# Moving head tails across partitions with a TensorE permutation instead of a DMA, with fewer filler matmuls and a new instruction order, in a fused linear-attention and feed-forward kernel

## The chip, the cores and the metric

The kernel runs on one core of a Trainium2 chip. The metric is the device time in microseconds of one execution, and lower is better. Several executions are timed; the median is given together with the lowest and the highest. One further execution is recorded by the hardware profiler, and all views below come from it. Engines are named as the profile names them: PE is TensorE (its matmuls), PEld its weight loads, DVE is VectorE, ACT is ScalarE, POOL is GpSimd, and SP is SyncE, which here only starts DMAs.

## The reference

Eight batches of eight heads, 576 positions and a head width of 64 go through a linear attention with a learned feature map. The result goes through a layer norm and a two-layer feed-forward block with a residual.

```python
def phi(x):
    proj = np.einsum('bhsd,df->bhsf', x, w_phi)            # 64 -> 128 features
    proj = proj - np.max(np.abs(proj), axis=-1, keepdims=True)
    return np.concatenate([np.exp(proj), np.exp(-proj)], axis=-1)
q_p, k_p = (phi(q), phi(k))
kv = np.einsum('bhsf,bhsd->bhfd', k_p, v)
z = np.sum(k_p, axis=2)
num = np.einsum('bhsf,bhfd->bhsd', q_p, kv)
den = np.einsum('bhsf,bhf->bhs', q_p, z)[..., None] + 1e-06
attn_out = num / den
...
# x: attn_out with the heads side by side, 8 x 576 x 512
mu = np.mean(x, axis=-1, keepdims=True)
var = np.mean((x - mu) ** 2, axis=-1, keepdims=True)
xn = (x - mu) / np.sqrt(var + 1e-06) * g_ln
ch = np.maximum(xn @ w_ch1, 0.0) @ w_ch2                   # 512 -> 2048 -> 512
return x + ch
```

## The kernel before

Work is tiled by pairs of batches. A pair has 1152 positions, which fill nine tiles of 128 rows. Tiles 0 to 7 hold 512 positions of each batch. Tile 8 is the mixed tile: its upper 64 rows are the last 64 positions of the first batch, its lower 64 rows those of the second. There are four pairs and 32 attention units, eight for each pair. A unit covers two (batch, head) combinations at once, one on each half of the partitions. For the first two pairs (`SPLIT`) a unit holds two neighbouring heads of the same batch; for the last two pairs it holds the same head of both batches.

A unit runs like this. Its q, k and v are loaded by SP (line 509, called by `load_main` and `load_tails`; the tails are the last 64 positions). q and k are transposed: for units 0 to 7 by PE (lines 645 and 653) with copies from PSUM by DVE or ACT (lines 660 and 662), from unit 8 on by a cast on DVE, ACT or POOL (lines 706 to 712, tile `b`) and a DMA transpose on SP (line 731). PE forms the projections `pk` (line 796), `pq` and `pt` and, for the tails, `px` (lines 754 and 755). DVE takes the row maxima `m`, ACT the exponentials `eb`, `ea` and `em`. v is scaled by an exponential into `vv` (lines 824 to 837), on POOL, or for the first units on POOL or DVE. PE accumulates the state in `n_bank` (lines 993 and 998), DVE or ACT copies it to `KV`, PE forms `num` (lines 1041 and 1047), DVE adds the two halves into `numc` (lines 1055 and 1060) and takes the reciprocal `rden` (line 1064), and POOL writes the quotient to `x` (line 1070).

In a unit of the first two pairs both heads belong to one batch, so on the mixed tile one of the two results comes out on the wrong half of the partitions. POOL writes that result to a small tile `xs`; after every fourth unit one DMA on ACT's queue (line 1130) moves the four collected results, 64 rows by 256 columns, to the other half of `x`. There are four such moves, two for each of the first two pairs.

When a pair's rows are complete, DVE takes the layer norm statistics (lines 1188 and 1203), the centred rows `xc` are transposed to `xT` (PE for the first pair, with g multiplied in through `ngln` at lines 1161 and 1163; DMA after that), and the feed-forward block runs. It is 832 matmuls for the hidden layer (`hT_ps`, line 1275), a relu on DVE or ACT (lines 1283 and 1285), 592 matmuls for the output (`ch_ps`, line 1305) and a final addition on DVE (line 1312).

The weights are loaded on POOL's queue, w1 in four parts at line 601 and w2 in four parts at line 612. Two small DMAs on SP (line 521) wait for a part of w1 or of w2, so that the loads behind them on SP start only then. g is loaded by SP at line 591, and DVE makes `ngln` of it at line 595.

The program order of every engine is written by a planner, the class `Order`. Each operation is added with its engine (or a choice of engines), an estimated duration, what it reads and writes, and the buffers that it takes or gives back. `run` plays the operations through in estimated time, and each engine takes the ready operation of lowest rank. A rank is a due time, worked back from the end, plus a correction from the table `OFF` for each kind of operation and unit. When PE has nothing ready before 36 us of planned time (`WARM`), the planner puts in a filler, a matmul of zeros with 120 columns (line 1503). A full DMA ring (`RING`) holds back further DMAs on it. The engines then run their lists strictly in this order.

PSUM has three pools: A (two buffers of two banks), N (one bank, `n_bank`, which the fillers write too) and B (three banks, for transposes, projections, `hT_ps` and `ch_ps`).

Of the kernel before, what the change touches and what calls it, by code (L numbers as in the profile page):

```python
# [10 lines left out]
FP32 = mybir.dt.float32  # L11
# [6 lines left out]
def bcast(ap: bass.AP, dim: int, n: int) -> bass.AP:  # L18
# [11 lines left out]
        0: 32.4, 1: -3.7, 2: 184.2, 3: -840, 4: -194.1, 5: -28.3, 6: -229.5, 7: 33.3, 8: 45,  # L30
        9: -539.6, 10: 152, 11: 166.5, 12: 510.5, 13: 780.4, 14: 17,
    },
    "gln": {
        0: -336.4,
    },
    "k": {
        0: -747.6, 1: 3.1, 2: 13.2, 3: 2336.4, 4: -153, 5: 169.6, 6: 3041.1, 7: -24.5, 8: -13.7,
        9: -121.2, 10: 2105.3, 11: -111.4, 12: -801.7, 13: 48.4, 14: 956.1,
    },
    "k.copy": {  # L40
        0: 303.5, 1: -156.1, 2: -30.4, 3: -67.5, 4: -25.5, 5: -23.1, 6: -8.4, 7: 126.8,
    },
    "k.em": {
        0: -36.2, 1: 16, 2: -30.2, 3: 2074.1, 4: -160.9, 5: 506.5, 6: 1498.1, 7: -115.7, 8: 487.3,
        9: -248.4, 10: -509.2, 11: -763.6, 12: 32.9, 13: -16.4, 14: 333.1,
    },
    "k.exp": {
        0: 892, 1: 680.1, 2: 913.8, 3: 1000, 4: -396.5, 5: 114.6, 6: 959.1, 7: 128.1, 8: 314.6,
        9: 1536.5, 10: -354.9, 11: -335.4, 12: -27, 13: -77, 14: 237.3,
    },  # L50
    "k.max": {
        0: -6661.7, 1: -16.8, 2: -277.6, 3: 22.3, 4: -472.7, 5: -30.2, 6: -31.4, 7: -186.7,
        8: -308.3, 9: -143.6, 10: -195.1, 11: 155.1, 12: -6149.9, 13: -3.3, 14: -6158.9,
    },
    "k.trans": {
        0: -97.2, 1: 108, 2: -53.9, 3: -186.6, 4: -480.3, 5: -159.3, 6: -450, 7: -38.7,
    },
    "kv": {
        0: 286.2, 1: 1059.8, 2: -466.3, 3: -37.1, 4: -180.5, 5: -17.5, 6: -549.1, 7: -227.7,
        8: -245.7, 9: -33.9, 10: -8.1, 11: 346.1, 12: 907.8, 13: -19.5, 14: -60.7,  # L60
    },
    "kv.copy": {
        0: 912.4, 1: 169, 2: 1552.3, 3: -226.4, 4: 572, 5: 112, 6: 1240.8, 7: 572, 8: 491.8,
        9: 1311.2, 10: 40.2, 11: 221.2, 12: 24.5, 13: -502.8, 14: 73.8,
    },
    "ln": {
        1: 301.8, 3: -104.9, 5: -6.6, 7: 128.2, 9: -561.5, 11: -849.4, 12: -1099, 13: 116.3,
        14: 10.6,
    },
    "load": {  # L70
        0: 158.8,
    },
    "mixed": {
        0: 35.8, 1: -185.8, 2: -16.9, 3: -86.7, 4: -229.1, 5: 195.3, 6: -90.5, 7: 455.9, 8: -949.2,
        9: -967.5, 10: -91.5, 11: 16.1, 12: 77.2, 13: -6043, 14: 448.4,
    },
    "mixed.exp": {
        0: 20.9, 1: 560.6, 2: 91.1, 3: -306.6, 4: 197, 5: -2.3, 6: 42.5, 7: 349.4, 8: 228.3,
        9: -167.6, 10: -376.7, 11: -109.3, 12: -155.8, 13: -167, 14: -28.1,
    },  # L80
    "mixed.max": {
        0: 65.3, 1: 102.8, 2: -327.8, 3: -962.8, 4: 211.4, 5: -1323, 6: 70.6, 7: -650, 8: 75.3,
        9: 1099.5, 10: 76.1, 11: -1098.5, 12: -90.7, 13: -715.7, 14: 529.6,
    },
    "num0": {
        0: 345.1, 1: -40.2, 2: -11.4, 3: 18, 4: -37.1, 6: 362.8, 7: 57.4, 8: 256.8, 9: -843.9,
        10: -49.5, 11: 591.4, 12: -1.8, 13: 963.9, 14: 184.1,
    },
    "num0.dve": {
        0: 101.2, 1: 2.8, 2: -67.5, 3: -245.5, 4: -32.1, 5: 407.7, 6: -61.4, 7: -245.2, 8: -405.8,  # L90
        9: -204.4, 10: 56.2, 11: 489.8, 12: -114.3, 13: -325.9, 14: -110.7,
    },
    "num0.put": {
        0: 415.1, 1: 56.4, 2: 23.3, 3: -82.8, 4: -553.5, 5: 481.8, 6: -1293.1, 7: 537.7, 8: -981,
        9: -845.9, 10: 128.5, 11: 74.2, 12: -1101.2, 13: 119.7, 14: -246.6,
    },
    "num1": {
        0: 1678.7, 1: 1611.5, 2: 204.2, 3: 8.1, 4: -173.6, 5: 22.3, 6: 448.5, 7: 1975.8, 8: -222.6,
        9: -54.5, 10: 13.7, 11: 39.8, 12: -1141.5, 13: -1220.2, 14: -1219,
    },  # L100
    "num1.dve": {
        0: 288.8, 1: 926.9, 2: 211.1, 3: 221.7, 4: -1480.5, 5: -121.2, 6: 7.4, 7: -321.5,
        8: -264.8, 9: -62.1, 10: -560, 11: -967, 12: -331.4, 13: -26.7, 14: 939.8,
    },
    "num1.put": {
        0: 763.2, 1: -18.1, 2: 211.3, 3: 3058.9, 4: 838.4, 5: 1781.7, 6: -13.1, 7: 830.5, 8: 749.5,
        9: 49.1, 10: -25.4, 11: 87.7, 12: -236.9, 13: 795.2, 14: 1071.9,
    },
    "q.copy": {
        0: 1413.7, 1: 594.3, 2: 486.8, 3: 263.7, 4: -71, 5: 12.4, 6: 148.6, 7: 195.7,  # L110
    },
    "q.em": {
        4: -274.3, 5: 1, 6: 27.6, 7: -502.7, 8: 29.8, 9: -502.3, 10: 65.2, 11: 494.7, 12: 761.6,
        13: 1224.5, 14: 52.8,
    },
    "q.max": {
        4: -11.4, 5: 178.1, 6: 2151.8, 7: -154.8, 8: 854.1, 9: -335.3, 10: 1738.2, 11: 296.6,
        12: -21.8, 13: -86.3, 14: 690.3,
    },
    "q.trans": {  # L120
        0: 136.7, 1: 242.2, 2: 16.5, 3: 122.9, 4: -6.8, 5: -19.6, 6: 91.3, 7: 27.9,
    },
    "q0": {
        0: 24.3, 1: 192.3, 2: 8.4, 3: -594.7,
    },
    "q0.em": {
        0: 34.4, 1: -74.9, 2: -376.1, 3: -208.6,
    },
    "q0.max": {
        0: 164.5, 1: 12.7, 2: 98.9, 3: -1420,  # L130
    },
    "q1": {
        0: -2210.5, 1: 15, 2: 17, 3: 1136.9,
    },
    "q1.em": {
        0: 2888.2, 1: -0.8, 2: 325.4, 3: 521.5,
    },
    "q1.max": {
        0: 360.6, 1: -0.1, 2: -2.6, 3: -49.7,
# [1401 lines left out]
```

## Time and profile before

| | us |
|---|---|
| median of 6 runs | 374.86 |
| lowest and highest | 373.31 and 377.55 |
| the profiled execution | 374.56 |
| its span, first to last instruction | 372.8 |
| first feed-forward matmul starts (line 1275) | 35.9 |
| first w2 load is issued (line 612) | 40.93 |
| last feed-forward matmul starts | 367.9 |
| four moves of `xs`, issue to landing | 3.3 to 5.1 |

The profile gives busy time for each engine; a "busy" PE is not a PE at its peak, since the ends of the pipelined matmuls are modelled. The chain of waits starts from the last instruction and is followed back, at each step to what released it or to the instruction before it on its engine. A view by stretch gives busy time in a window chosen by the reader. In the groups of instructions one row stands for all instructions of a line, engine and tile, with their count, the busy time, the mean duration of one, and the idle time of the engine just before them.

### The profile page before, as it was taken

The numbers are of one execution on the slowest core, as the hardware profiler recorded it, in microseconds if no ns is written. First come the engines' busy times: TensorE is split into PE (matmuls) and PEld (weight loads), VectorE is DVE, ScalarE is ACT, GpSimd is POOL, SyncE is SP. The second block draws the span as 40 slices with busy tenths as digits, with TensorE's granted clock in tenths as the row PEclk, the third lists the DMA queues.
The fourth block names the chain that finished last, engine by engine and source line by source line (L and its number), as shares of the span: only waits on it lengthen the run. The fifth ranks groups of instructions, "written<-read, shape, count | busy, mean of one in ns | idle before, by whom it ended". The sixth has DMA issues, their size and how long they took to land.

```text
span 372.8 us, 9348 instructions
## 1 busy us (share of the span) xinstructions
PE 360.0 (97%) x3548; PEld 230.3 (62%) x3548; DVE 292.4 (78%) x645; ACT 239.1 (64%) x569; POOL 176.2 (47%) x356
## 2 busy tenths in 40 slices
PE   8899998999999999979999999999999999999995
PEld 8899775666556566646656646666666555555543
DVE  6899988979599899979988898868687955454522
ACT  4898876567889999979779789835574630000000
POOL 2644848637668878746586664161727100000000
PEclk9999999999999999999999999999999999999999
DMA  6999699995999997696943448500100180200102
GB/s 181 268 199 299 118 217 270 251 263 136 258 256 222 240 282 197 162 196 156 216 91 85 119 108 178 109 27 6 58 0 31 45 196 1 57 29 30 56 28 87
DMA packets 92975, 53.38 MB, mean 143 GB/s; under 512 B 59393, under 2 KB 88449, under 8 KB 92929
## 3 DMA queue, kind: packets, MB, share of 16 engines
q1 hardware_dynamic: 87040, 48.19, 51.8%
q0 software_dynamic: 4224, 4.19, 7.1%
q10 hardware_dynamic: 1664, 0.39, 0.6%
q8 instruction: 28, 0.46, 0.5%
q14 instruction: 19, 0.15, 0.1%
HBM read 36.77 MB, written 9.44 MB: 124 GB/s over the span
## 4 chain that ended last, share of the span: by engine, by line
PE 70%; DMA 14%; ACT 6%; DVE 5%; SPq 2%; issue 1%; POOL 1%; ACTq 0%; DVEq 0%; POOLq 0%
PE ch_ps L1305 27%; PE hT_ps L1275 27%; DMA qkT<-b 6%; DMA qk<-in_k_dram 4%; PE n_bank L998 3%; PE num L1041 2%; PE pk L796 2%; PE pq L941 2%; SPq L509 2%; DMA w<-in_moe_w_ch_dram 2%; ACT eb L812 2%; DMA x<-xs 1%; PE pt L946 1%; ACT xc L1212 1%; DVE numc L1055 1%
## 5 line engine op out<-in xcount | busy, mean ns | idle before, releaser
L1275 PE MATMUL hT_ps<-xT,w 128*128 128x384 bf16 (+1 forms) x832 | 150.7, 313 | 2.6 <-DVE hT L1283 1.1
L1305 PE MATMUL ch_ps<-w,hT 128*128 128x512 bf16 (+1 forms) x592 | 146.2, 373 | 0.3 <-ACT hT L1285 0.3
L1275 PEld LDWEIGHTS <-w 128*128 128x128 bf16 x832 | 76.7, 98 | 49.6 <-issue 6.4
L1283 DVE TENSOR_SCALAR hT<-hT_ps 128x384 bf16<-128x384 f32 (+1 forms) x134 | 70.6, 530 | 42.2 <-PE hT_ps L1275 40.4
L1305 PEld LDWEIGHTS <-hT 128*128 128x128 bf16 x592 | 54.4, 98 | 45.8 <-issue 1.8
L1070 POOL TENSOR_TENSOR x<-numc,rden 128x192 bf16<-128x192 f32 (+4 forms) x112 | 49.6, 461 | 65.3 <-DVE rden L1064 60.2
L824 POOL TENSOR_TENSOR vv<-v,em 128x512 bf16<-128x512 f32 x59 | 61.7, 1048 | 29.7 <-ACT em L809 15.6
L812 ACT ACTIVATE eb<-pk 128x1024 bf16<-128x1024 f32 x64 | 65.0, 1046 | 7.5 <-DVE m L802 7.5
L1285 ACT ACTIVATE hT<-hT_ps 128x384 bf16<-128x384 f32 (+1 forms) x74 | 34.5, 471 | 53.9 <-PE hT_ps L1275 53.0
L965 ACT ACTIVATE ea<-pt 128x1024 bf16<-128x1024 f32 x56 | 57.5, 1039 | 11.9 <-PE pt L946 11.1
L802 DVE TENSOR_REDUCE m<-pk 128x8 f32<-128x1024 f32 x32 | 38.7, 1212 | 1.4 <-PE pk L796 1.4
L958 DVE TENSOR_REDUCE m<-pq 128x8 f32<-128x1024 f32 x28 | 34.1, 1218 | 2.9 <-PE pq L941 2.6
L1312 DVE SCALAR_TENSOR_TENSOR o<-ch_ps,rstd,x 128x512 f32<-128x512 f32 (+1 forms) x37 | 27.0, 731 | 10.6 <-PE ch_ps L1305 8.6
L1041 PEld LDWEIGHTS <-ea 128*128 128x128 bf16 x512 | 25.3, 97 | 7.2 <-issue 0.7
L1188 DVE BATCH_NORM_STATS2 st<-x 128x6 f32<-128x256 bf16 (+1 forms) x52 | 25.0, 514 | 2.6 <-DMA x<-xs 2.0
L998 PE MATMUL n_bank<-vv,eb 128*128 128x65 bf16 x512 | 26.8, 194 | 0.0
L712 POOL TENSOR_TENSOR b<-qk,one 128x512 bf16<-128x512 f32 x20 | 20.6, 1041 | 9.9 <-DMA qkT<-b 8.8
L837 POOL TENSOR_TENSOR vv<-vx,em 128x130 bf16<-128x130 f32 x60 | 24.2, 403 | 0.0
L998 PEld LDWEIGHTS <-eb 128*128 128x128 bf16 x512 | 22.3, 98 | 2.7
L1503 PE MATMUL n_bank<-wz 128*128 128x120 bf16 x295 | 23.4, 229 | 0.5 <-ACT KV L1007 0.5
L1212 ACT ACTIVATE xc<-x,mv 128x512 bf16<-128x512 bf16 x30 | 20.2, 722 | 2.6 <-DVE mv L1203 1.9
L1503 PEld LDWEIGHTS <-wz 128*128 128x128 bf16 x295 | 19.6, 105 | 1.1 <-issue 0.8
(92 smaller groups left out, 457.6 us busy)
## 6 DMA issues: line engine op xcount, KB each, us to landing
out_dram<-o SPq DMA_DIRECT2D x31, 256.0 KB, 2.8
qk<-in_k_dram SPq DMA_DIRECT2D x24, 256.0 KB, 4.2
v<-in_v_dram SPq DMA_DIRECT2D x24, 256.0 KB, 3.5
qk<-in_q_dram SPq DMA_DIRECT2D x24, 256.0 KB, 4.8
w<-in_moe_w_ch_dram POOLq DMA_DIRECT2D x8, 512.0 KB, 11.4
qk<-in_k_dram SPq DMA_DIRECT2D x4, 512.0 KB, 6.4
qk<-in_q_dram SPq DMA_DIRECT2D x4, 512.0 KB, 6.7
v<-in_v_dram SPq DMA_DIRECT2D x4, 512.0 KB, 5.0
```

Source lines behind the costliest of these rows:

```text
L802: nc.vector.reduce_max(out=u["m"][:, 1, 0:MX], in_=u["pk"], axis=AX.X, apply_absolute_value=True)
L812: nc.scalar.activation(u["EB"][:, t, 0:MX, :], u["pk"], AF.Exp, scale=(1.0, -1.0)[t])
L824: eng.tensor_tensor(out=u["vv"][:, t, 0:MX, 0:D], in0=vb[:, hh, :].rearrange("p (c d) -> p c d", d=D), in1=bcast(e[:, 0:MX], 2, D), op=ALU ...
L958: nc.vector.reduce_max(out=out, in_=ps, axis=AX.X, apply_absolute_value=True)
L965: nc.scalar.activation(u["EA"][:, t, :], u["pt", None], AF.Exp, scale=(1.0, -1.0)[t])
L998: nc.tensor.matmul(ps[:, t, c // 4, :], EB[:, t, c, :], vv[:, t, c, :], start=False, stop=(t == 0 and c == MX - 1), skip_group_check=True,)
L1070: nc.gpsimd.tensor_tensor(out=dst, in0=st["numc"][ps_, at, 0:D], in1=bcast(st["rden"][ps_, at], 2, D), op=ALU.mult,)
L1275: nc.tensor.matmul(st["ps"], w1_sb[:, kc, jj * P : (jj + 1) * P], xT_bufs[xj][:, kc : nt * KC : KC, :], start=(kc == 0), stop=(kc == KC - 1),)
L1283: nc.vector.tensor_relu(h_sb[:, 0 : nt * P], st["ps"])
L1285: nc.scalar.activation(h_sb[:, 0 : nt * P], st["ps"], AF.Relu)
L1305: nc.tensor.matmul(ch[t, c][:, cols], hT[jj][:, rt * P : (rt + 1) * P], w2_sb[:, jj, cols], start=(jj == 0), stop=(jj == JC - 1),)
L1503: nc.tensor.matmul(warm, wz, wz[:, 0:WN], start=False, stop=False, skip_group_check=True)
```

## The change

- The result on the wrong half of the mixed tile is moved by PE. There are now two tiles `xs`, one for each batch of a pair, full height and zeroed once. A 128 x 128 matrix `swap`, the identity with its halves exchanged, is made by two copies on POOL. One matmul of 256 columns puts the rows on the other half in PSUM (pool B), and DVE or ACT copies 64 rows of it to `x`. The DMA on ACT's queue is gone. In the new order three of the four copies are on ACT and one is on DVE.
- Of the fillers that the planner would put in after 8 us of planned time only every fourth is emitted; the others leave PE idle for that time. The program has 116 fillers in place of 296 (the opening matmul of the same shape included).
- g's load is placed before the tails of units 4 to 7 in SP's list, and its entry in `OFF` is gone.
- The planner's figures for DMAs are changed: several active rings slow each other by 12%, POOL's ring may hold twice as much, and three durations are lower.
- `OFF` holds other numbers throughout, so the order differs on every engine. Matmuls of hidden layer and output placed ahead of a unit's `pk`: unit 9, 168 and 64 before, 128 and 32 after; unit 16, 300 and 144 before, 284 and 126 after; unit 31, 596 and 348 before, 536 and 306 after. Of the large `vv` products of units 0 to 3 five stood on DVE and three on POOL; now one stands on DVE and seven on POOL.

```diff
 OFF = {
     "en": {
-        0: 32.4, 1: -3.7, 2: 184.2, 3: -840, 4: -194.1, 5: -28.3, 6: -229.5, 7: 33.3, 8: 45,
+        0: 106.4, 1: 177.1, 2: 8.4, 3: -631.1, 4: -363.1, 5: 6.8, 6: -683.7, 7: -315.3, 8: -1773,
...
-    "gln": {
-        0: -336.4,
     },
...
-        wait, held = None, 0.0
+        wait, held, spare = None, 0.0, 0
...
                 turn += rings[k][0][1]
+            turn *= 1.0 + 0.12 * (len(active) > 1)
...
-                    full = op.dma and out.get(op.dma[0], 0.0) + op.dma[1] > self.RING
+                    full = op.dma and out.get(op.dma[0], 0.0) + op.dma[1] > self.RING * (1 + (engine == "POOL"))
...
                     if engine == "PE" and 1.0 <= now < self.warm:
                         op = Op()
-                        op.emit, op.engine, op.engines, op.number = self.filler, "PE", ("PE",), -1
+                        op.emit, op.engine, op.engines, op.number = None, "PE", ("PE",), -1
+                        spare += 1
+                        if now < self.COLD or spare % 4 == 0:
+                            op.emit = self.filler
...
-    xs = consts.tile([P, 4, D], BF16, name="xs")
+    xs = [consts.tile([P, 4, D], BF16, name=f"xs{i}") for i in range(2)]
+    for xs_ in xs:
+        nc.vector.memset(xs_, 0.0)
+    swap = consts.tile([P, P], BF16, name="swap")
+    for i in range(2):
+        nc.gpsimd.tensor_copy(
+            out=swap[:, i * 64 : i * 64 + 64], in_=ident[:, 64 - i * 64 : 128 - i * 64]
+        )
...
-                ns=0.05 if n < EARLY else 0.047,
+                ns=0.05 if n < EARLY else 0.043,
...
-            w=[("w1", n, kc) for kc in range(KC)] + [("w1 came", n)], us=0.75, ns=0.1)
+            w=[("w1", n, kc) for kc in range(KC)] + [("w1 came", n)], us=0.75, ns=0.094)
...
-        dma("POOL", V, 512, emit, r=gate, w=[("w2", n)], us=0.75, ns=0.1)
+        dma("POOL", V, 512, emit, r=gate, w=[("w2", n)], us=0.75, ns=0.094)
...
-                        put(xs[ps_, i : i + 1, :], ps_, slice(nt - 1, nt))
+                        put(xs[b][ps_, i : i + 1, :], ps_, slice(nt - 1, nt))
...
                     if i == 3:
-                        def move(ps_=ps_, half=half):
-                            nc.scalar.dma_start(
-                                out=u["x"][b * 64 : b * 64 + 64, MX, :].rearrange(
-                                    "p (i two d) -> p i two d", two=2, d=D
-                                )[:, :, half, :],
-                                in_=xs[ps_],
-                            )
-
-                        dma("ACT", V_put, 256, move, r=[("xs", b, j) for j in range(4)],
-                            w=[("x", pair, MX, 2 * j + half) for j in range(4)], ns=0.019)
+                        rows = slice(b * 64, b * 64 + 64)
+
+                        def move():
+                            st["swap"] = ps_B.tile([P, 4, D], FP32, tag="B", name="swap_ps")
+                            nc.tensor.matmul(st["swap"], swap, xs[b], start=True, stop=True)
+
+                        def moved(engine, half=half):
+                            dst = u["x"][rows, MX, :].rearrange(
+                                "p (i two d) -> p i two d", two=2, d=D
+                            )[:, :, half, :]
+                            if engine == "DVE":
+                                nc.vector.tensor_copy(out=dst, in_=st["swap"][rows])
+                            else:
+                                nc.scalar.copy(out=dst, in_=st["swap"][rows])
+
+                        key = ("swap", pair, b)
+                        add("PE", mm(1, 256), V, move, r=[("xs", b, j) for j in range(4)],
+                            w=[key], acquire=[("B", 1)])
+                        add(("DVE", "ACT"), (0.33, 0.3), V_dve, moved, r=[key],
+                            w=[("x", pair, MX, 2 * j + half) for j in range(4)], release=[("B", 1)])
...
+    load_weights(order)
     for key in "kqv":
         load_tails(key, 4, next(order), "SP")
-    load_weights(order)
```

## The prediction

> **What bounds the kernel now.** I read the engine shares and the forty slices first, then the busy time by stretch, then the chain of waits, then the waits inside the two stretches where TensorE has gaps. The slices:
>
> ```profile
> PE 360.0 (97%) x3548; PEld 230.3 (62%) x3548; DVE 292.4 (78%) x645; ACT 239.1 (64%) x569; POOL 176.2 (47%) x356
> PE   8899998999999999979999999999999999999995
> DVE  6899988979599899979988898868687955454522
> ACT  4898876567889999979779789835574630000000
> ```
>
> TensorE looks full, but until 36 us much of that is filler: the matmuls of line 1503 compute nothing. By stretch (columns: length, then busy us and instructions of PE, PEld, DVE, ACT, POOL, then the clock, DMA share, GB/s):
>
> ```profile
> 8.00:36.00 28.00, 26.80 (x491) 25.21 (x489) 25.53 (x66) 25.13 (x76) 14.09 (x29) 1.00 1.10 257
> 36.00:60.00 24.00, 22.18 (x263) 17.75 (x260) 21.39 (x51) 18.43 (x46) 16.21 (x34) 1.00 0.96 197
> 140.00:160.00 20.00, 20.00 (x211) 12.03 (x210) 19.03 (x44) 19.30 (x47) 15.06 (x33) 1.00 0.70 182
> 160.00:180.00 20.00, 18.03 (x201) 11.63 (x199) 17.55 (x36) 17.93 (x46) 10.52 (x20) 1.00 0.85 189
> 200.00:240.00 40.00, 40.00 (x398) 24.31 (x397) 36.43 (x79) 35.00 (x80) 20.90 (x37) 1.00 0.54 124
> ```
>
> So there are two regimes. From 8 to 36 us DVE (25.5 of 28) and ACT (25.1 of 28) carry the head; PE only fills. From 200 us on PE is full with the feed-forward matmuls and nothing but less PE work or an earlier start can help. Between them PE has holes: 1.8 us in 36 to 60, and 2.0 us in 160 to 180 between two full stretches. The chain of waits (start, us, what) names a cause for the head and for the second hole:
>
> ```profile
> 13.31 0.38 PE n_bank L1503 x7
> 14.15 0.58 PE n_bank L1503 x8
> ...
> 27.08 1.10 PE n_bank L1503 x18
> 28.18 0.25 PE num L1041 x8
> 28.43 0.06 PE qxT_ps L653
> 28.49 0.58 PE n_bank L1503 x11
> ...
> 158.32 5.10 DMA x<-xs
> 163.42 0.02 issue
> 163.44 0.69 DVE st L1188
> ```
>
> Fillers stand on the chain: 18 of them, 1.10 us, lie before a num product although the KV copy it needs had ended at 27.04. The waits of 156 to 170 us (total, times, longest):
>
> ```profile
> DVE st L1188 <- DMA x<-xs: 2.0, 1, 2.0
> PE n_bank L993 <- DVE numc L1060: 1.7, 1, 1.7
> ```
>
> The move of xs is issued at 158.32 and lands after 5.1 us; the statistics stand at the head of DVE's queue, DVE is idle 2.0 us, the numc behind them is late, and PE waits 1.7 us for it at 166.81.
>
> **What the Trainium skill says.** "DMA: Bandwidth & Descriptors", section "Latency and other measured facts", has a fixed cost of about 2 us for a DMA, mostly the receipt round trip; here a 32 KB move took 3.3 to 5.1 us, the trace is dearer. "Trainium Kernel Development and Optimization", section "Key Constraints": GpSimd cannot access PSUM, so the new copy out of PSUM must be DVE's or ACT's, as the diff has it; no run here shows the limit itself. "TensorE: Matmul & The Clock Gate", section "What's actually happening": the array falls to half clock after an idle window of some 3.4 us. The trace has no such fall after warming up: four matmuls of 384 columns take 0.65 us on the chain, 162 ns each, the full-clock pace.
>
> **The change, part by part.** Sums are made against the profiled execution, 374.56 us (span 372.8); the median of the six runs is 0.3 us higher.
>
> *The permutation.* Removed: four DMAs on ACT's queue, 0.60 to 0.69 us of issue each (2.5 us of ACT), landing 3.3 to 5.1 us. Added: four matmuls of 256 columns; the nearest row is px, 0.11 us on the chain, so 0.44 us of PE; four copies of 256 columns, three on ACT and one on DVE in the new order; nearest row the KV copy of 260 columns, 0.38 (ACT) and 0.43 (DVE). ACT gains about 1.3 us, DVE pays 0.4. For the last of the four: the put ends at 157.95, matmul, copy and hand-offs need about 0.8 us, so the statistics could run from 158.8, not 163.4: more than the 2.0 us that DVE waits. numc moves up by 2.0 us, to PE's need at 164.8, while PE has hT work until 165.1, so the hole closes; next late is then PE itself. Worth 2.0 - 0.44 = 1.5 us; bounds 2.0, and -0.4 if another late value holds the same hole. The change adds a wait: PE's swap matmul waits for POOL's put, and all of PE's queue stands behind it, where before only ACT's queue did. It takes one of three B buffers meanwhile. In the new order the shortest stretch between a unit's last products and its swap (the second one) holds 2.7 us of PE work; numc twice, reciprocal and put need 0.35 + 0.35 + 0.12 + 0.29 = 1.1 us when DVE and POOL are free. I count it at nothing; a late put costs its lateness.
>
> *Fillers and the new head.* Fillers fall from 296 to 116, nearly all after the first 8 us. The fillers on the chain between 11.9 and 30 us sum to 3.0 us; three quarters of that is 2.3 us. They matter only if DVE and ACT can follow. Counted in program order, up to the eighth reciprocal (units 0 to 3 complete, the event behind the last put and behind w2's load at 40.93), DVE loses four vv products, two qkT copies, one KV copy, one tail copy and one xT, and gains two memsets:
>
> ```profile
> L824 DVE TENSOR_TENSOR vv<-v,em 128x512 bf16<-128x512 f32 x5 | 3.5, 706 | 0.3 <-ACT em L809 0.2
> L660 DVE COPY qkT<-qkT_ps 128x512 bf16<-128x512 bf16 x8 | 3.3, 415 | 0.4 <-PE qkT_ps L645 0.4
> L662 ACT COPY qkT<-qkT_ps 128x512 bf16<-128x512 bf16 x6 | 3.6, 607 | 0.9 <-PE qkT_ps L645 0.9
> L824 POOL TENSOR_TENSOR vv<-v,em 128x512 bf16<-128x512 f32 x4 | 4.2, 1071 | 6.4 <-DVE m L883 6.3
> ```
>
> 4 x 0.706 + 2 x 0.415 + 0.43 + 0.22 + 0.34 - 0.28 = 4.4 us less on DVE (the other rows of the same view give 0.43, 0.22, 0.34; the memsets are half of ex's 0.272 each). ACT up to its sixteenth ea gains two qkT copies, a KV copy and a small em and loses two px pairs and a tail copy: 1.21 + 0.38 + 0.28 - 1.26 - 0.27 = +0.3 us; it idled 2.9 us of 8 to 36, so it allows at most 2.5. POOL takes the four vv, two copies for the permutation matrix and one put: 4 x 1.071 + 0.4 + 0.3 = 5.0 us, beside 13.9 us of idle in 8 to 36. DVE allows 4.4, ACT 2.5, the fillers give 2.3: I take 2.3. Upper bound 4.4. Lower bound -0.6: up to its fourth relu ACT has 2.9 us more (three qkT copies, KV, tail copy, xT), which would outweigh 2.3 if the first feed-forward products waited for those relus.
>
> *Edits at nothing.* g's load goes ahead of six tails: 0.60 us of SP's queue. It landed at 31.8 and is read at 34.0, nothing waited; the tails, issued by 18.4, are used from 28.4 on. Without that cover, 0.6. On POOL the first w1 load now stands behind two more vv and the copies, less a small pair: 2.14 + 0.4 - 0.86 = 1.7 us later; it frees the loads of units 4 on (gate at 25.65, then some 4.2 us to land, 30.7), used at 35.6: 5 us of cover. w2's load, behind the puts, moves up with the head. The larger POOL ring and the changed DMA figures act only through the order.
>
> *The new order after 60 us.* It changes no work but places attention earlier. Ahead of unit 9's k product stand 168 hT and 64 ch matmuls before, 128 and 32 after; of unit 16's 300 and 144, then 284 and 126; of unit 31's 596 and 348, then 536 and 306. Each of these matmuls has to run anyway, so I take nothing; it can close part of the 1.8 us hole after 36 us, or open new ones: +1.8 to -7, the second being the rival below.
>
> Sum: 374.56 - 1.5 - 2.3 = 370.8 in the profile, 371.1 on the median.
>
> **The rivals.**
> Only the permutation pays (0.17): ACT holds the head, as its +0.3 and +2.9 say, and the fillers' room becomes plain idle time. For it: ACT is 90% busy there. Against: the chain has fillers directly after a finished KV copy. 374.9 - 1.5 = 373.4.
>
> Unit 9's transpose comes late (0.20; slower). Its DMA transpose is issued at 76.97 now and its product runs at 87.5; in the new order the product stands only 2.4 us of PE work after unit 8's, now at 71.1, so with the head 2.3 us earlier it is due at about 71.2, and with the transposes' median landing of 4.1 us the issue must come by 67.1, 9.9 us sooner. PE takes its queue in order, so it stands still for what is missing, and SP's later loads stand behind the transpose too. For it: SP is in order and that chain is 18% transposes from 62 to 125 us. Against: the q and k for units 8 and 9 are there at 57.25 already. If the issue comes only 3 us sooner PE stands 6.9 us: 371.1 + 6.9 = 378.0. It decides from 3.8 us of lateness on.
>
> The array cools (0.08; slower): with some 60 fillers left from 8 to 36 us, 3 us of them and under 15 us of real work leave PE idle 10 of 28 us. If the idle time bunches into such a window, some 6 us of real PE work on the head's chain double: 377. Against: no gap of a whole window is left between units.
>
> **How the numbers follow.** Forecast 371.1 (0.55), its own range 368.5 to 373.5 from the bounds above. A measurement of this kernel tells 0.5% from nothing: under 373.0 is faster, over 376.7 slower. Faster: 0.48 from the forecast, 0.07 from the permutation-only case, 0.03 from a transpose only a little late: 0.58. Same: 0.07 + 0.07 + 0.02 = 0.16. Slower: the rest of the transpose case, 0.15, the cold array, 0.08, and 0.03 of the permutation-only case with a late put: 0.26. The range 367.5 to 378.5 leaves out half of the cold case, the far end of the transposes and the low end where DVE's whole 4.4 us pay: about 0.2.
>
> **What would show it.** Permutation: no DVE wait for x, and 160 to 180 us at 20.0 of PE. Head: no long runs of fillers on the chain, w2's load at about 38.6, not 40.9. Wrong if ACT ends its sixteenth ea where it does now, at 33, if PE waits at unit 9 for the transpose, or at a swap for POOL, or if fillers late in the head take twice their 53 ns.

## The result and the profile after

| | before | after |
|---|---|---|
| median, us | 375.63 (70 runs) | 373.13 (33 runs) |
| lowest and highest, us | 372.47 and 380.01 | 370.54 and 375.91 |
| ratio after to before, 95% interval | | 0.994 (0.9923 to 0.9956) |
| the profiled execution, its span, us | 374.56, 372.8 | 375.61, 373.8 |

The change saves 0.6%, some 2.2 to 2.5 us; 3.8 us were forecast. The profiled execution of the changed kernel is one of its longest, so lengths in its profile are compared stage by stage only, and a second profile of the same kernel (span 370.7 us) stands beside it below. The page of the profile after, with the slices of PE, DVE, ACT and the clock granted to TensorE:

```profile
PE 355.7 (95%) x3372; PEld 223.7 (60%) x3372; DVE 294.8 (79%) x652; ACT 236.2 (63%) x560; POOL 184.4 (49%) x366
PE   8787899999999999899799999999999999999995
DVE  5989997998999897889778889888788945454532
ACT  3989887796999997787476879876553710000000
PEclk9989999999999999999989999999999999999999
```

PE has 176 matmuls fewer: 180 fillers gone, four permutations added. The clock, which had no gap after warming up before, now has two, at slices 3 and 21. By stretch (length, then busy us and instructions of PE, PEld, DVE, ACT, POOL, then clock, DMA share, GB/s), after:

```profile
8.00:36.00 28.00, 20.97 (x305) 17.29 (x303) 25.63 (x60) 26.15 (x78) 18.68 (x35) 0.94 1.13 281
36.00:60.00 24.00, 22.34 (x275) 18.14 (x275) 22.96 (x57) 21.32 (x54) 16.04 (x35) 1.00 0.87 175
140.00:160.00 20.00, 18.88 (x180) 10.67 (x179) 16.73 (x39) 16.06 (x38) 13.23 (x28) 1.00 0.87 216
160.00:180.00 20.00, 19.77 (x214) 12.24 (x213) 18.34 (x40) 15.53 (x37) 14.38 (x25) 1.00 0.89 227
...
16.90:20.30 3.40, 1.56 (x25) 1.30 (x24) 2.19 (x4) 3.40 (x9) 3.37 (x6) 1.00 1.08 173
20.30:23.70 3.40, 3.39 (x42) 2.99 (x40) 3.40 (x6) 2.99 (x9) 2.61 (x5) 0.50 1.22 200
184.10:187.50 3.40, 1.43 (x15) 0.80 (x14) 1.01 (x4) 2.60 (x9) 2.18 (x3) 1.00 0.00 0
187.50:190.90 3.40, 3.40 (x32) 1.93 (x30) 1.80 (x5) 1.40 (x4) 3.23 (x7) 0.51 0.00 0
```

In 8 to 36 us PE is 5.8 us less busy, as it should be without fillers. DVE is as busy as before (25.63 against 25.53), although four large vv products and two copies of qkT have left it, and ACT is busier (26.15 against 25.13). The stretch from 160 to 180 us is nearly full, but 140 to 160, full before, has lost 1.1 us. The last four rows show each cool window with the one ahead of it: where PE worked only 1.56 or 1.43 of 3.40 us, the next 3.40 us ran at half clock. PE's waits from 140 to 200 us (total, times, longest), after:

```profile
PE n_bank L1049 <- ACT ex L779: 2.0, 1, 2.0
PE n_bank L1001 <- POOL vv L832: 1.1, 1, 1.1
```

The wait for numc that stood at 166.81 us is gone. Two others have come: for a product that POOL scales, ending at 153.9 us, and for an exponential of ACT, ending at 186.6 us.

How much of this counts is read from one sum: from the start of each matmul to the start of the next, less the time of that matmul in an unbroken run, is either filler or loss. Loss includes the slowing in cool windows. Useful matmul work is 331.2 us before and 331.7 us after, and the sums in us are:

| kernel (profiled execution) | fillers and loss to 60 us | loss 60 to 200 us | first hT | last matmul | span |
|---|---|---|---|---|---|
| before | 24.6 | 9.1 | 35.9 | 367.9 | 372.8 |
| after | 24.6 | 10.7 | 37.0 | 369.7 | 373.8 |
| after, second profile (`e9_after_again`) | 25.0 | 7.3 | 37.4 | 366.7 | 370.7 |
| old order with both parts (`e15_before_both_again`) | 22.4 | 5.9 | 34.4 | 363.2 | 367.7 |
| after, DVE and ACT relieved (`e13_pool_copies`) | 23.7 | 8.6 | 36.1 | 366.9 | 371.0 |
| the same and q, k loaded earlier (`e14_pool_copies_gate`) | 22.8 | 8.1 | 34.8 | 365.2 | 369.2 |

Each row is one execution. The forecast wanted 22.3 in the first column and about 7.1 in the second. The second profile of the changed kernel has the second, at 7.3; the first profile, with its cool window at 187.5 us, has 10.7. The first column did not fall in either, so the time that is missing in both is in the head, up to 60 us.

### The profile page after: what moved, and what is told of

Read it like the earlier page. It is cut to its first block, busy times and chain, and to the rows that moved or that the text cites. A ratio compares the mean times of both kernels' runs of the same rounds, so it can differ in the third digit from the quotient of the medians.

```text
span 373.8 us, 8992 instructions
## 1 busy us (share of the span) xinstructions
PE 355.7 (95%) x3372; PEld 223.7 (60%) x3372; DVE 294.8 (79%) x652; ACT 236.2 (63%) x560; POOL 184.4 (49%) x366
## 4 chain that ended last, share of the span: by engine, by line
PE 70%; DVE 10%; ACT 8%; DMA 6%; POOL 3%; issue 2%; SPq 1%; DVEq 0%; POOLq 0%; ACTq 0%
PE hT_ps L1293 28%; PE ch_ps L1323 26%; DMA qkT<-b 3%; PE n_bank L1006 3%; ACT eb L820 3%; PE pk L804 3%; DMA out_dram<-o 2%; PE num L1049 2%; PE pq L949 2%; DVE st L1206 1%; PE pt L954 1%; DVE m L810 1%; PE n_bank L1521 1%; DVE m L966 1%; POOL vv L832 1%
## 5 line engine op out<-in xcount | busy, mean ns | idle before, releaser
L1293 PE MATMUL hT_ps<-xT,w 128*128 128x384 bf16 (+1 forms) x832 | 152.7, 313 | 0.5 <-DMA xT<-xc 0.2
L1323 PE MATMUL ch_ps<-w,hT 128*128 128x512 bf16 (+1 forms) x592 | 149.7, 374 | 0.0
L1301 DVE TENSOR_SCALAR hT<-hT_ps 128x384 bf16<-128x384 f32 (+1 forms) x144 | 75.8, 528 | 43.6 <-PE hT_ps L1293 42.2
L832 POOL TENSOR_TENSOR vv<-v,em 128x512 bf16<-128x512 f32 x63 | 66.1, 1050 | 21.0 <-issue 12.4
L1303 ACT ACTIVATE hT<-hT_ps 128x384 bf16<-128x384 f32 (+1 forms) x64 | 29.4, 462 | 69.0 <-PE hT_ps L1293 68.9
L820 ACT ACTIVATE eb<-pk 128x1024 bf16<-128x1024 f32 x64 | 66.0, 1046 | 4.1 <-DVE m L810 3.7
L1049 PEld LDWEIGHTS <-ea 128*128 128x128 bf16 x512 | 25.1, 98 | 10.7 <-issue 3.8
L720 POOL TENSOR_TENSOR b<-qk,one 128x512 bf16<-128x512 f32 x25 | 25.7, 1041 | 8.1 <-DMA qkT<-b 6.6
L1006 PE MATMUL n_bank<-vv,eb 128*128 128x65 bf16 x512 | 27.7, 197 | 0.6 <-ACT eb L820 0.6
L1049 PE MATMUL num<-KV,ea 128*128 128x65 bf16 x400 | 19.2, 194 | 1.3 <-DVE numc L1068 0.9
L1063 DVE TENSOR_TENSOR numc<-num,em 128x390 f32<-128x390 f32 (+2 forms) x36 | 19.2, 534 | 1.6 <-PE num L1049 1.2
```

Source lines behind the costliest of these rows:

```text
L820: nc.scalar.activation(u["EB"][:, t, 0:MX, :], u["pk"], AF.Exp, scale=(1.0, -1.0)[t])
L832: eng.tensor_tensor(out=u["vv"][:, t, 0:MX, 0:D], in0=vb[:, hh, :].rearrange("p (c d) -> p c d", d=D), in1=bcast(e[:, 0:MX], 2, D), op=ALU ...
L1006: nc.tensor.matmul(ps[:, t, c // 4, :], EB[:, t, c, :], vv[:, t, c, :], start=False, stop=(t == 0 and c == MX - 1), skip_group_check=True,)
L1049: nc.tensor.matmul(ps[t][:, i, :], ea(u, t, c), KV[:, t, c // 4, :], start=True, stop=True,)
L1293: nc.tensor.matmul(st["ps"], w1_sb[:, kc, jj * P : (jj + 1) * P], xT_bufs[xj][:, kc : nt * KC : KC, :], start=(kc == 0), stop=(kc == KC - 1),)
L1301: nc.vector.tensor_relu(h_sb[:, 0 : nt * P], st["ps"])
```

## The experiments

Each ran beside the kernel before on the same chip; ratios are to that, with their 95% intervals, and the times are medians (runs in brackets). All of them compute the whole result.

**All fillers back in the changed kernel.** The order is unaltered.

```diff
-                        if now < self.COLD or spare % 4 == 0:
+                        if now < self.COLD or spare % 1 == 0:
```

> The changed kernel with every filler kept (317 in place of 116), all other instructions in the same order. Theory 'the array cools': with the gaps left open the clock drops to half for one or two stretches of 3.4 us in most executions; with all fillers its mean stays at 0.998 or more and the time falls by about 1 us, to 371.5 to 372.5. Theory 'fillers on the chain' (the prediction's): fillers delay real matmuls, so keeping them costs up to 2.3 us, to 374 to 375.5. Theory 'ACT holds the head': no change, 373.1.

Measured 374.04 us (22), ratio 0.9997 (0.9979 to 1.0016). Next to 0.994 for the changed kernel, fewer fillers are worth 0.57% in the new order, about 2.1 us. But by unit 8's `pk` the two differ little: it starts at 71.0 us with all fillers and at 70.4 and 70.8 in the two profiles of the changed kernel. So at most 0.6 us of the 2.1 lies in the head. The rest appears later, in its profile between the `pk` of units 8 and 20, which are 104.4 us apart with all fillers and 102.2 and 100.8 in the changed kernel, in waits that differ from execution to execution; why is not settled.

**A quarter of the fillers in the kernel before.** Its order is unaltered.

```diff
-                        op.emit, op.engine, op.engines, op.number = self.filler, "PE", ("PE",), -1
+                        op.emit, op.engine, op.engines, op.number = None, "PE", ("PE",), -1
+                        spare += 1
+                        if now < self.COLD or spare % 4 == 0:
+                            op.emit = self.filler
```

> The kernel before with a quarter of its later fillers (109 in place of 296), all other instructions in the same order. 'Fillers on the chain': faster by 2.3 us, to 373.3. 'The array cools': clock below 0.998 in most executions, slower by 0.5 to 2 us, 376 to 377.5. 'ACT holds the head': 375.6, no change.

Measured 373.74 us (22), ratio 0.997 (0.9948 to 0.9992): 0.3%, 1.1 us. Its profile has the first hT at 34.6 us (35.9 before) and unit 8's `pk` at 69.1 (71.1): in the old head the edit brings 2.0 us. At unit 31's `pk` 0.7 us of it is left. In 10 of its 22 executions the mean clock was under 0.997, so the array cooled in these.

**The permutation in the kernel before,** in the place of the DMA, with the copy on ACT; the two tiles `xs` and the matrix are made as in the change.

```diff
-                            nc.scalar.dma_start(
+                            ps = ps_B.tile([P, 4, D], FP32, tag="B", name="swap_ps")
+                            nc.tensor.matmul(ps, swap, xs[b], start=True, stop=True)
+                            rows = slice(b * 64, b * 64 + 64)
+                            nc.scalar.copy(
```

> The kernel before with the permutation in the place of each DMA move, the order otherwise the same. 'The permutation pays': DVE's wait for x at 160 us goes, PE busy 19.5 or more of 160 to 180, faster by 1.5 us, 374.1. Rival 'the hole has another cause': same, 375.6, or slower by 0.4 us for the added PE work.

Measured 373.73 us (22), ratio 0.9985 (0.9967 to 1.0003): 0.6 us, not surely different from nothing by time, and at most 1.2 by its interval. In its profile unit 20's `pk` comes at 176.1 us instead of 177.3 and unit 31's at 274.9 instead of 276.5.

**The DMA back in the changed kernel,** at the place of the copy, without the matmul.

```diff
-                            st["swap"] = ps_B.tile([P, 4, D], FP32, tag="B", name="swap_ps")
-                            nc.tensor.matmul(st["swap"], swap, xs[b], start=True, stop=True)
...
+                            nc.scalar.dma_start(out=dst, in_=xs[b][ps_])
```

> The changed kernel with the DMA move at the place of the permutation's copy and without its matmul, the order otherwise the same. 'The permutation pays': slower by 1.5 us or more (the readers stand where a quick copy was planned), 374.6 to 377. Rival 'it pays nothing': 372.7 to 373.1.

Measured 374.39 us (22), ratio 0.9982 (0.9959 to 1.0004); against 0.994 the permutation is worth 0.42%, 1.6 us, in the new order.

**The new order alone:** all fillers and the DMA, the two edits above together.

> The new order by itself: the changed kernel with every filler kept and with the DMA move in the place of the permutation's copy. Theory 'the head's DVE saving is eaten by waits for POOL': first feed-forward matmul at about 37.5 us (35.9 before), time no better than before, 374.5 to 376. Rival 'the new order shortens the head, as predicted': 372.5 to 374, first feed-forward matmul before 35.5.

Measured 377.05 us (11), ratio 1.0065 (1.0041 to 1.0089). The order by itself is 2.4 us slower. Part of that belongs to the DMA, which lands late for readers that were placed behind a quick copy: DVE's statistics wait 3.6 us for it. PE's waits from 145 to 195 us in this kernel:

```profile
PE n_bank L1049 <- DVE o L1326: 2.5, 1, 2.5
PE n_bank L1001 <- DVE numc L1068: 1.8, 1, 1.8
```

These 4.3 us are 2.2 more than the same stretch had before (1.7 for numc and 0.4 for an exponential). Between this kernel and the one above it the fillers alone differ, and the times by 0.83%, though unit 8's `pk` starts at 70.3 us in both: again the fillers' cost is not in the head.

**Both parts in the old order,** the edits of the second and third experiment together, run on two chips.

> The kernel before with the permutation in the place of each DMA move and a quarter of the later fillers, its own order kept. If the gain is made by these two and not by the new order: as fast as the changed kernel or faster, 372.5 to 373.2, first feed-forward matmul at 34.6. If the new order carries the gain: 374 or more.

> The kernel before in its own order with the permutation and a quarter of the later fillers, a second time. The theory that both parts are worth in the old order what was forecast (3.8 us in all, first hT at 34.4 us) and that the new order takes some of it back expects a ratio to before near 0.990 again, and nothing here slower than the changed kernel (0.991 to 0.994). The rival, that its five executions were lucky, expects 0.994 or more.

Measured 371.68 us (5), ratio 0.9909 (0.9877 to 0.994), and 371.10 us (6), ratio 0.989 (0.9852 to 0.9927). The forecast's 3.8 us of 374.86 would be a ratio of 0.990. The rows by stretch of the second of these:

```profile
8.00:36.00 28.00, 21.45 (x318) 17.56 (x319) 26.40 (x70) 26.52 (x80) 14.99 (x31) 1.00 1.13 269
36.00:60.00 24.00, 23.27 (x269) 17.80 (x267) 22.51 (x55) 19.79 (x48) 17.37 (x34) 1.00 0.94 204
160.00:180.00 20.00, 20.00 (x237) 13.42 (x234) 18.89 (x39) 19.00 (x47) 13.26 (x25) 1.00 0.96 221
```

The stretch from 160 to 180 us is full, PE has 1.1 us more in 36 to 60, and DVE and ACT are busier in the head than before because the same work ends sooner. The time of both parts was there to be had without the new order. It is more than the 0.3% and 0.15% that each part brought alone in this order. The clock may be a part of that: none of these eleven executions had a mean clock under 0.997. No run takes this apart.

**Waits between DVE and POOL.** In the new head DVE's small vv instructions and `ngln` take several times as long as before. The groups of the first 45 us, in the kernel before and then, of the first 42 us, in the changed one (line, engine, operation, shapes, count, busy us, mean ns):

```profile
L837 DVE TENSOR_TENSOR vv<-vx,em 128x130 bf16<-128x130 f32 x4 | 1.2, 288 | 0.0
L833 DVE CAST vv<-em 128x8 bf16<-128x8 f32 x4 | 1.1, 281 | 0.0
L595 DVE TENSOR_SCALAR ngln<-gln 128x4 f32<-128x4 f32 x1 | 0.1, 135 | 0.0
```

```profile
L845 DVE TENSOR_TENSOR vv<-vx,em 128x130 bf16<-128x130 f32 x4 | 2.9, 717 | 0.0
L841 DVE CAST vv<-em 128x8 bf16<-128x8 f32 x4 | 2.6, 650 | 0.0
L603 DVE TENSOR_SCALAR ngln<-gln 128x4 f32<-128x4 f32 x1 | 1.0, 1005 | 0.0
```

Nine instructions take 6.5 us where they took 2.4, so of the 4.4 us that were to leave DVE 4.1 came back. The Trainium skill states the mechanism ("SBUF — State Buffer", section "Who interferes with whom"): GpSimd and certain VectorE instructions share a pair of ports, whichever issues first holds it for its whole instruction, and the other blocks fully. The trace agrees: five of the nine last 1.0 to 1.2 us, the length of one large vv on POOL (1081 ns there), and four of these five end 0.03 to 0.16 us after such a product does. The fifth, a cast at 17.85 us, lasts on through the DMA issue that follows the product on POOL. I took this for the cause and tried to remove it in two ways. First the small products go to POOL and `ngln` to ACT:

```diff
-            eng = nc.gpsimd if engine == "POOL" else nc.vector
+            eng = nc.gpsimd
...
-            "DVE", 0.1, rk("gln", 0), lambda: nc.vector.tensor_scalar_mul(out=ngln, in0=gln_sb, scalar1=-1.0),
+            "DVE", 0.1, rk("gln", 0), lambda: nc.scalar.activation(ngln, gln_sb, AF.Copy, scale=-1.0),
```

> The changed kernel with the four small pairs of vv operations that stand on DVE in the head moved to POOL at the same places, and ngln made by ACT; all else in the same order. 'Waits for POOL': DVE drops the 6.2 us that these nine operations took (1.9 at their bare durations), first feed-forward matmul 1 to 2 us earlier than the changed kernel's 37.0, time 371.5 to 372.5. Rival 'ACT holds the head': 373.1, first feed-forward matmul at 36.5 or later.

Then instead the three large products of units 0 and 1 that had gone to POOL return to DVE (`PORT = (0, 1)`):

```diff
-            eng = nc.gpsimd if engine == "POOL" else nc.vector
+            eng = nc.gpsimd if engine == "POOL" and n not in PORT else nc.vector
```

> The changed kernel with the large vv products of units 0 and 1 (three of them) moved from POOL back to DVE at the same places. 'Waits for POOL': DVE gains 3 x 0.7 = 2.1 us of work, but its small vv operations beside them fall from 1.15 us to 0.29, so the first feed-forward matmul stays within 0.5 us of 37.0 or comes earlier. Rival 'the small operations are long for another reason': they stay at 1.15 us and the head grows by 2 us.

They gave 371.58 us (5), ratio 0.9914 (0.989 to 0.9939), and 371.20 us (4), ratio 0.9903 (0.9867 to 0.9939), both a little better than 0.994 by their middle values. A second round, with the changed kernel itself and the second of these two side by side on another chip, corrected that:

> The changed kernel unaltered, run beside the next two kernels on one chip. The theory that the new head gave its gain back in waits between DVE and POOL expects it 1 to 2 us behind the kernel with the large vv products of units 0 and 1 on DVE (371.2 us before, so some 372.5 to 373.3 here); in executions without a fall of the clock about 372.6. The rival, that the difference between 373.1 and 371.2 was one of chips or of chance, expects the two within 0.5 us here.

> The changed kernel with the three large vv products of units 0 and 1 on DVE, a second time beside the changed kernel itself. Theory: 1 to 2 us faster than the changed kernel (ratio to before 0.989 to 0.992, against 0.994). Rival of chance: the same as the changed kernel within 0.5 us.

The changed kernel gave 372.03 us (6), ratio 0.9909 (0.9874 to 0.9944); with the large products on DVE it gave 372.46 us (16), ratio 0.9928 (0.9902 to 0.9953). No difference. The waits themselves did go: with the large products on DVE the four small products last 284 ns each again, and the casts 434 instead of 650; `ngln` alone still takes 1.0 us. Freeing DVE does not help much either: with the small products on POOL its busy time in 8 to 36 us falls from 25.63 to 20.25 us, and the first hT still comes only at 36.5 (37.0 and 37.4 in the changed kernel). So the waits are real and cancel DVE's saving, but they are at most a small part of the missing time.

**Half of the fillers,** with the large products on DVE.

```diff
-                        if now < self.COLD or spare % 4 == 0:
+                        if now < self.COLD or spare % 2 == 0:
```

> As the one before, but every second filler after 8 us is emitted and not every fourth. If the falls of the clock cost more than the saved fillers bring, this is 0.3 to 1 us faster than with a quarter, with fewer falls; if the saved PE time is what counts, it is 0.4 us slower (a third of the 1.3 us that all to a quarter saved), with the number of falls of no weight.

Measured 373.31 us (22), ratio 0.9954 (0.9935 to 0.9972), 0.85 us slower than with a quarter. Four of 22 executions had a mean clock under 0.997, against 7 of 16. The cool windows are rarer with more fillers, and it does not pay.

**What holds the new head.** The chain of waits of the changed kernel just ahead of the first hT:

```profile
33.36 0.12 DVE mv L1221
...
33.56 0.72 ACT xc L1230
34.28 0.15 ACT qkT L670
34.44 0.20 ACT rstd L1237
...
34.87 0.36 ACT xT L1181
35.23 0.17 ACT eb L775
35.40 0.17 ACT ex L779
...
36.24 0.17 ACT eb L775
36.40 0.18 ACT ex L779
36.58 0.04 issue
36.62 0.38 PE qkT_ps L653 x4
37.01 0.05 PE n_bank L1521
37.06 0.96 PE hT_ps L1293 x8
```

For 3.0 us ACT stands on the path almost without a gap. PE's next transpose waits until ACT has read the tails' projections (PE's waits of 8 to 60 us put 1.2 us down to `ex`), and the first hT stands behind that transpose in PE's queue. Ahead of this the chain runs on DVE, from 28.5 to 33.5 us, but ACT has next to no room there: from 25 to 36 us it is busy 10.75 of 11 us (10.39 in the second profile, 9.75 in the kernel before). Where DVE was freed the same place looks different, in the kernel with the small products on POOL:

```profile
30.77 5.41 DMA qk<-in_q_dram
36.17 0.37 PE qkT_ps L653 x4
36.55 0.05 PE n_bank L1521
36.60 0.96 PE hT_ps L1293 x8
```

The profile puts this wait down to a load of q that has only just landed. I believed it, took ACT and this load for two limits within half a microsecond of each other, and made three kernels to take them one by one; what they say of the load comes at their end. First the small DMA on SP that holds those loads back waits for the first part of w1, not the second (the order is unaltered):

```diff
-        src = w1_sb[0:1, 0, n * WC : n * WC + 8] if key == "w1" else w2_sb[0:1, n * JC // NW, 0:8]
+        src = w1_sb[0:1, 0, 0:8] if key == "w1" else w2_sb[0:1, n * JC // NW, 0:8]
```

> The changed kernel, its order unaltered; the small DMA on SP that holds the loads of q and k of units 4 on back waits for the first part of w1 and no longer for the second. If those loads, which land at about 36.2 us and whose transposes stand ahead of the first hT in PE's queue, hold the new head, the first hT (37.0 to 37.4 us) comes up to 1 us sooner, the time falls by as much. If ACT holds it (ACT 26.15 us busy of 28), the first hT stays within 0.3 us, and so does the time.

Measured 372.49 us (9), ratio 0.9922 (0.9893 to 0.9951), first hT at 37.05 us: no change, as for a head that ACT holds. Next, on top of the small products on POOL, ACT's six large copies of the head go to DVE:

```diff
-            copy(engine, u["qkT"][:, cols], u["qkT_ps", cols.start // 512])
+            copy("DVE" if u["n"] < 5 else engine, u["qkT"][:, cols], u["qkT_ps", cols.start // 512])
```

> The kernel with the small vv pairs on POOL and ngln on ACT, and in addition the six qkT copies of 512 columns that ACT has in the head go to DVE (6 x 0.66 = 4.0 us off ACT, 6 x 0.42 = 2.5 us onto DVE, which had 20.3 of 28 us). If ACT's load holds the new head, the first hT comes before 36.0 us (36.5 before); if the loads of q and k do, it stays at 36.3 to 36.6 us, with PE waiting for a q or k load just ahead of it, and the time stays at 371.6 within 0.7 us.

Measured 370.88 us (9), ratio 0.9897 (0.9863 to 0.9931), first hT at 36.14 us. That lies between the two expectations; the chain has no load in it there, it is ACT's from 27.7 to 35.7 us. And both edits:

> Both of the two edits before together. If ACT and the loads hold the head in turn, only this one brings the first hT down to 35.5 us or less, 1.5 to 2 us sooner than the changed kernel, and the time to about 370.5. If neither does, it stays above 36.3.

Measured 370.82 us (6), ratio 0.9889 (0.985 to 0.9927), first hT at 34.80 us, 2.2 us sooner than in the changed kernel. The chain of waits of this kernel at the same place:

```profile
32.68 0.36 ACT xT L1181
33.04 0.17 ACT eb L775
...
34.21 0.17 ACT ex L779
34.39 0.04 issue
34.43 0.38 PE qkT_ps L653 x4
34.81 0.05 PE n_bank L1521
34.87 0.96 PE hT_ps L1293 x8
```

The same chain, 2.2 us earlier, and fillers and loss to 60 us fall from 24.6 to 22.8, nearly the 22.3 of the forecast. It looks as if ACT and the loads held the head in turn. The traces say that it was ACT each time, and never the loads:

- The transpose ahead of the first hT is that of unit 4's k. That load landed at 30.7 us in the kernel with the small products on POOL, 5.4 us before it was used. The q that the profile names is unit 6's, which raises the same semaphore; it happened to land just when the wait ended. With ACT's copies moved it landed at 35.98 us, and in this last kernel at 36.91, while the transposes had started at 35.77 and 34.43.
- In all these kernels the transpose starts 0.05 us after ACT's last `ex` has ended: at 36.57 us in the changed kernel, 36.11 with the small products on POOL, 35.72 with the copies moved, 34.38 in the last one.
- The gate is not what brought the last step, from 36.14 to 34.80 us. It opens at 21.5 us in the last kernel, whose lead of 1.3 us is there at 20.6 already. This execution began sooner, with its first `pk` at 4.96 us against 5.90, which is chance as far as the profiles show. The medians, 370.88 and 370.82, are the same.

What ACT's copies cost is therefore read between executions that began alike: 0.85 us of first hT from the changed kernel to the one with the copies moved (first `pk` at 5.90 in both), 1.7 us from the kernel with the small products on POOL to the last one (5.00 and 4.96). DVE's relief is in the first of these figures, too. These are single profiles, so the size is rough.

By their medians three kernels stand at 0.989 to 0.991: both parts in the old order, and the last two. Their intervals part them neither from each other nor from the second round of the changed kernel, 0.9909. Both parts in the old order never ran beside the changed kernel on one chip; that this order is the better one rests on the medians and on the sums for the head, 22.4 against 24.6 and 25.0.

## Why the prediction was right and wrong

**The permutation: right in its mechanism, about right in size.** Forecast 1.5 us. No DVE wait for x is left on the chain, and undoing it in the new order costs 1.6 us. The loss from 60 to 200 us fell by 1.8 us in the second profile (1.4 after the 0.44 us of added matmuls); in the first, with its cool window, it rose by 1.6. In the old order the permutation brought 0.6 us alone and 2.3 to 3.0 beside fewer fillers, so its worth depends on what stands around it. The copies cost what the row of KV said; the changed kernel's instructions on the permutation's result (nanoseconds lowest, middle, highest):

```profile
L1141 PE MATMUL swap_ps<-xs,swap x4: 269/270/273, 40.8 to 154.9; 128*128 128x256 bf16 x4
L1150 ACT CAST x<-swap_ps x3: 367/368/390, 41.4 to 120.1; 64x256 bf16<-64x256 f32 x3
L1148 DVE CAST x<-swap_ps x1: 428/428/428, 155.2 to 155.2; 64x256 bf16<-64x256 f32 x1
...
  POOL xs L1078: 0.6, 1
```

The wait that it adds, PE for POOL's put, came once, for 0.6 us.

**The fillers in the new head: the step that failed.** It said "DVE allows 4.4, ACT 2.5, the fillers give 2.3: I take 2.3". The fillers' 2.3 was well sized: in the old order the same edit moved unit 8's `pk` by 2.0 us and, with the permutation, fillers and loss to 60 us by 2.2. In the new order it did not arrive in the head: that sum is 24.6 and 25.0 where it was 24.6, nothing to -0.4, and putting all fillers back moves unit 8's `pk` by 0.2 to 0.6 us only. The two allowances were wrong. DVE's 4.4 us were counted at durations from the kernel before, where POOL had four fewer large products beside DVE, and 4.1 us came back as waits for POOL. ACT's allowance was its idle time, 2.5 us, as if it could be used anywhere; but its work stands in a row ahead of the first hT, with 0.25 and 0.61 us of idle time from 25 to 36 us, and the first hT starts 0.42 us after that row's last `ex` in every kernel of the new order that is compared here. The same step's lower bound named this: 2.9 us more on ACT up to its fourth relu would outweigh the fillers "if the first feed-forward products waited for those relus". It was ACT's load, though not the relus, that they waited for, by way of a transpose ahead of them in PE's queue. What came lies by that lower bound, -0.6; the likeliest value was taken from the other end. Two of the signs that the prediction named say the same: ACT ended its sixteenth `ea` at 33.2 us, as before (33.3), and the first w2 load was issued at 40.7, not at 38.6. By time, fewer fillers were worth 2.1 us in the new order, too; as most of that lies behind the head, for a reason that stays open, it does not bear the forecast's reasoning out.

**g and w1: nothing, as forecast.** The cover before was smaller than the step had it: unit 4's k took 5.8 us to land, not some 4.2, so it was there at 32.3 us and not at 30.7. In the changed kernel it landed at 30.1, 6.5 us before its transpose. Opening the gate earlier moved neither the first hT nor the time of the changed kernel (37.05 and 372.49 us).

**The later order: taken at nothing, mixed.** With all fillers and the DMA it cost 2.4 us by itself. It opened the two waits that end at 153.9 and 186.6 us and shortened the end: from the last matmul to the end of the span 4.9 us before, 4.1 in the second profile. The old order with both parts loses 5.9 us from 60 to 200, the new one 7.3 and 10.7.

**The rivals.** "Only the permutation pays" (373.4) gave as its reason that ACT holds the head. That reason was right, and 373.13 was measured. That the time fits so well is partly luck: the new order has a cost of its own, and fewer fillers did bring time, behind the head. Unit 9's transpose was not late: its `pk` runs at 72.9 us, 2.5 us after unit 8's, and PE has no wait there. The array does cool, in 19 of 34 executions of the changed kernel by mean clock under 0.997, against 17 of 75 of the kernel before in one set of runs. It did not cost 6 us: the medians of those with none, one and more cool windows are 372.60, 373.13 and 375.24 us. It turned no gain into a loss and added some 0.5 us to the median.

## What to carry to other kernels

Taking filler off an engine pays only as far as the next engine on the same path gives way, and what that engine allows is not its idle time but the run of its instructions ahead of the event that counts: follow that run through the queue, with what stands in front of it. When work is moved from DVE to POOL, the instructions left on DVE must be priced beside a busy POOL; here the move was worth nothing. A wait that a profile puts down to a load should be held against another run: a load that lands after the instruction has started cannot be what it waits for. And a lead between two profiles belongs to an edit only if it begins where the edit can act. A new order that comes with two good edits should be tested apart from them; here the edits in the old order brought all of the forecast.

## What the runs showed of the hardware

The Trainium skill ("TensorE: Matmul & The Clock Gate", section "What's actually happening") has the array fall to half clock after an idle window of some 3.4 us. Here it fell after windows in which PE was busy 1.56 and 1.43 of 3.40 us, 46% and 42%, and stayed at full clock after every other window of the same raster from 10 us on, of which the least busy had 2.49 of 3.41, 73%. Other profiles narrow this down. In the second profile of the changed kernel the fall at 21.4 us came after a window with 1.70 of 3.41 us (50%), and one with 1.94 (57%) had none behind it; with half of the fillers the window that ended at 154.9 us had 1.72 of 3.41 and no fall behind it either. So the window ahead of a fall need not be idle, as the page has it: here it was enough that PE's busy time, as the profile models it, fell to half of it. Each of these falls lasted one window of 3.4 us. So fillers need not fill, but a head without them must not drop to half.

DVE's small casts and products, 0.18 and 0.29 us each where nothing holds them up, last 1.0 to 1.2 us when one has to wait for a two-input product on POOL. The wait does not show as idle time but as a longer instruction, and in the mean of a row it is mixed with the short ones: the four casts of the changed kernel's row last 180, 186, 1197 and 1039 ns.
